# Inverting softmax denominators before their transpose, moving one GpSimd difference a pair forward, and reordering three ScalarE steps at the end of attention

## The chip, the core and the metric

One NeuronCore of one Trainium2 chip runs the whole program. The metric is the device time of one execution in microseconds; "before" is the median of three runs. Engines are named as in the profile: PE (TensorE), PEld (its weight loads), DVE (VectorE), ACT (ScalarE), POOL (GpSimd), SP (SyncE, which only issues DMAs).

## What is computed

Clustered attention over 2 batches, 8 heads, 768 positions and head size 64, and then two gated MLPs on 1536 tokens of width 512 (hidden widths 2048 and 1536):

```python
q_assign = argmax(q_n @ c_n);  k_assign = argmax(k_n @ c_n)
mask   = q_assign[:, :, :, None] == k_assign[:, :, None, :]
scores = where(mask, scale * q @ k.T, -1e9)
attn   = exp(scores - max(scores));  attn /= sum(attn) + 1e-9
x = attn @ v                      # heads side by side: 1536 x 512
h = x @ w_in;  x = (h * sigmoid(h)) @ w_out
out = (sigmoid(x @ w_gate) * (x @ w_val)) @ w_out2
```

## The kernel before

**Attention** goes over 8 pairs p of heads (NPAIR = 8: pairs 0 to 3 are batch b = 0, pairs 4 to 7 batch 1). A pass p has 12 steps, one for each 128 x 768 tile of queries. Step i of pass p issues the scores of the tile two further on (L502, tile s in PSUM, two buffers), so tile 5 of a pair is issued in step 3 and tile 7 in step 5. DVE takes each tile's maximum (L510, `nm`), ACT the exponential with the row's sum (L515, `e`, sums in `tot`), PE turns the result (tiles `t`, L544, and `u`, L531), ACT and DVE copy it out (`ph`, L66 and L69), and PE multiplies by the values (L581, `v`), of which ACT copies one half (L596, `other`) and DVE adds the two (L600, `xf`). PE's order is written out by hand. In attention the order of DVE, ACT, POOL and SP is made by a planner, which places ready instructions by the order in which they were traced; `tc.issue_after(x)` only keeps an instruction behind x in its own engine's queue. Each queue runs in order.

**The next pairs' inputs** are prepared beside this by `prep`: POOL splits q and k in a high and a low part (`qh`, `ql` L431, `kh`, `kl` L434), and DVE picks the clusters: `mk`, `eq`, `wq` (all traced under L456) between the maxima of tiles 4 and 5, and a second `mk` and `oh` after tile 7.

**The end of a pair** is `finish(p)`, a generator that advances by one step in each step of pass p + 1, from step 3 on. For pairs 0 to 5 it waits two steps, then PE turns the 128 x 12 sums to 12 x 128 (L621, `pr`), DVE adds 1e-9 and inverts from PSUM (L627, L628, `rt`), and SP writes `rt` to DRAM and reads it back spread over partitions (L696, L698, `rb`). POOL scales the pair into `acc` (L634). Pair 6 already goes another way: add and reciprocal on the 128 x 12 sums in SBUF (L615, L616, `rs`), then the transpose, then a copy by ACT (L624). Pair 7 has `finish_last`. The three PSUM tiles of `ps_t` are shared by `t`, `u`, `pr` and others.

**POOL also prepares the first MLP's right operands** of batch 0: quarters of `acc` and differences of quarters (`xt1` = b12 - b11 and so on, L648) are rounded (L68) and their remainders taken (L82). They are traced in `finish(3)` behind named POOL instructions, the first difference behind the split of pair 6.

**The MLPs** use a seven-product scheme (`strassen`): x, w, X, y, z, v, W for the first block. X adds to the PSUM bank of x, so it waits until ACT has copied x out (`u2`, L1045). `two` rounds weights on ACT (L66) and takes the remainder on POOL (L880): for the first block `wi0s` and `wi0t` are the sums and differences of its quarters. `right_quarter("x", 1, q, ACT, DVE)` rounds two quarters of batch 1 on ACT and takes their remainders on DVE (L82).

Of the kernel before, what the change touches and what calls it, by code (L numbers as in the profile page):

```python
# [10 lines left out]
F32 = mybir.dt.float32  # L11
# [3 lines left out]
AF = mybir.ActivationFunctionType  # L15
# [17 lines left out]
def clustered_attention_then_two_mlps(ctx, tc, qT, kT, v, cen, cenT, w1i, w1o, w2g, w2v, w2o, out):  # L33
    nc = tc.nc
# [23 lines left out]
    begin = []  # L58
    maxima = []
    copied, latest, moved, firsts, added, paced = [], [], [], [], [], []  # L60
    cast_last = []
    home = {0: xp}

    def cast(eng, o, i):
# [22 lines left out]
    def right_quarter(name, b, q, caster, subber):  # L87
        right_operand(name, b, q, quarters(b)[q], caster, subber, "t1" if q == "12" else None)
# [54 lines left out]
    with ExitStack() as att:  # L143
# [430 lines left out]
        def values(p, j, g, pool=None, apart=False):  # L574
# [29 lines left out]
            one_half()  # L604
            both_halves()

        def finish(p):

            b, hp = divmod(p, HP)
            t = tots.pop(p)  # L610
            early = p == NPAIR - 2
            if early:
                rs = fin.tile([P, 2 * NT], F32, tag="rs", name=f"rs{p}")
                with tc.issue_after(maxima[(p + 1) * 2 * NT + GT + 1].ins):
                    nc.vector.tensor_scalar_add(t, t, 1e-9)  # L615
                    nc.vector.reciprocal(rs, t)  # L616
            else:
                yield
                yield
            pr = ps_t.tile([P, 512], F32, tag="t", name=f"pr{p}")  # L620
            nc.tensor.transpose(pr[0 : 2 * NT, 0:P], rs if early else t, ident)  # L621
            rt = fin.tile([P, P], F32, tag="rt", name=f"rt{p}")
            if early:
                nc.scalar.activation(rt[0 : 2 * NT], pr[0 : 2 * NT, 0:P], AF.Copy)  # L624
            else:
                with tc.issue_after(maxima[(p + 1) * 2 * NT + 2 * GT + 1].ins):
                    nc.vector.tensor_scalar_add(rt[0 : 2 * NT], pr[0 : 2 * NT, 0:P], 1e-9)  # L627
                    nc.vector.reciprocal(rt[0 : 2 * NT], rt[0 : 2 * NT])  # L628
            yield
            rb = fin.tile([P, S], F32, tag="rb", name=f"rb{p}")  # L630
            dma_rows(rb, rt)
            yield
            parts = [t.rearrange("p (h s) -> p h s", h=2) for t in (xf.pop(p), rb)]
            on_pool["scaled", p] = nc.gpsimd.tensor_tensor(acc[:, hp, :, b, :], *parts, op=ALU.mult)  # L634
            yield
            if b < B - 1 and hp == HP - 1:

                def temporary(name):
                    return wk.tile([P, KQ, HS], F32, tag="tt", name=name)

                b11, b21, b12, b22 = quarters(b).values()
                pool = nc.gpsimd
                t = {n: temporary(f"xt{n}{b}") for n in (1, 2)}

                def minus(o, a, c):
                    if o not in t:
                        t[o] = temporary(f"xt{o}{b}")
                    pool.tensor_tensor(t[o], a(), c(), op=ALU.subtract)  # L648

                def operand(n):  # L650
                    right_operand("x", b, f"t{n}", t[n], pool, pool)

                def quarter(q):
                    right_quarter("x", b, q, pool, pool)

                for key, todo in (
                    (("scaled", p), (partial(quarter, "11"), partial(quarter, "21"))),
                    (("split", p + 3), (partial(quarter, "22"), partial(minus, 1, lambda: b12, lambda: b11))),
                    (("scaled", p + 1), (partial(minus, 2, lambda: b22, lambda: t[1]), partial(operand, 1))),
                    (("split", p + 4), (partial(operand, 2), partial(minus, 4, lambda: t[2], lambda: b21))),  # L660
                    (("scaled", p + 2), (partial(operand, 4), partial(minus, 3, lambda: b22, lambda: b12), partial(operand, 3))),
                ):
                    while key not in on_pool:
                        yield
                    for one in todo:
                        with tc.issue_after(on_pool[key].ins):
                            one()
                        yield
# [117 lines left out]
        values(p, 1, 0, ps_t)  # L786
        late, early = turned(p, 1, GT + 1)
        early()
        late()
        late, early = turned(p, 1, GT + 2)  # L790
        late()
# [82 lines left out]
    def two(src, name, pool=None, after=()):  # L874

        w = (pool or buffer(name)).tile([P, 2, src.shape[1]], R32, tag="w", name=f"w{name}")
        hi, lo = w[:, 0], w[:, 1]
        with tc.issue_after(after[0].ins) if after else nullcontext():
            cast(nc.scalar, hi, src)
        nc.gpsimd.tensor_tensor(lo, src, hi, op=ALU.subtract)  # L880
        return hi, lo
# [12 lines left out]
    def scheme(a, b, name, all_four=False):  # L894

        a11, a12, a21, a22 = a[:, 0:Q], a[:, Q:], b[:, 0:Q], b[:, Q:]
        first = two(a, f"{name}a")
        t = wp.tile([P, 4, Q], F32, tag="s", name=f"s{name}", bufs=1)
        sub = nc.gpsimd.tensor_tensor
        sub(t[:, 0], a21, a22, op=ALU.add)  # L900
        sub(t[:, 1], t[:, 0], a11, op=ALU.subtract)
        sub(t[:, 2], a11, a21, op=ALU.subtract)
        sub(t[:, 3], a12, t[:, 1], op=ALU.subtract)
        after = latest if all_four else ()
        s12 = two(t[:, 0:2].rearrange("p a b -> p (a b)"), f"{name}s", after=after)
        s34 = two(t[:, 2:4].rearrange("p a b -> p (a b)"), f"{name}t", after=after)
        last = two(b, f"{name}b") if all_four else two(a22, f"{name}d", dp)
        made = dict(
            a11=part(first, 0),
            a12=part(first, 1),  # L910
            s1=part(s12, 0),
            s2=part(s12, 1),
            s3=part(s34, 0),
            s4=part(s34, 1),
            a22=part(last, 1 if all_four else 0),
        )
        if all_four:
            made["a21"] = part(last, 0)
        return made
# [93 lines left out]
    def strassen(w, name, take, bs, order="xyzwXvW"):  # L1013
# [22 lines left out]
        def column(n):  # L1036
            c[n] = temporary(f"{name}{n}")[:, bs]
            return c[n]

        for n in order:  # L1040
            if n == "x":
                o[n] = bank(f"{name}x", ppa)
                with tc.issue_after(ends[1].ins) if order[1] == "w" else nullcontext():
                    q = run(o[n], "a11", "11")
                nc.scalar.activation(column("u2"), q, AF.Copy)  # L1045
            elif n == "y":
                add(c["u2"], run(bank(f"{name}y"), "s2", "t2"), c["u2"])
            elif n == "z":
# [231 lines left out]
    def steps(main, beside=iter(()), n=None):  # L1280

        for _ in main:
            next(beside, None)
            if n is not None:
                n -= 1
                if n == 0:
                    return
# [18 lines left out]
    weights("1i", 0)  # L1306
    for q in ("11", "12"):
        right_quarter("x", 1, q, POOL, POOL)
    for q in ("21", "22"):
        right_quarter("x", 1, q, ACT, DVE)  # L1310
    front = hidden(0, ONE[0], "xwXyzvW")
    steps(front, n=1)
    look[0] = AHEAD
    weights("1i", 0)
    steps(front, n=5)
# [187 lines left out]
```

## Time and profile before

| | us |
|---|---|
| median of three runs (771.91 to 773.53) | 772.39 |
| the profiled execution | 770.78 |
| its span in the trace | 769.0 |
| PE busy in the span | 755.4 (98%) |
| DVE busy | 601.4 (78%) |
| ACT busy | 427.6 (56%) |
| POOL busy | 385.4 (50%) |

The profiled execution has 1.8 us outside its span. Attention takes the first 240 us, the MLPs the rest. Times in the trace count from the start of the span. "Pass 4" is the time in which pair 4's scores are issued. A number in square brackets at the end of a timeline row is the time that the engine sat idle before that instruction, and what ended it.

### The profile page before, as it was taken

The page shows a single profiled execution, that of the slowest core. Times are in us where ns is not written, and L with a number is a line of the kernel's source. Part 1 is how long each engine was busy: PE and PEld are TensorE (multiplying, and loading weights), DVE is VectorE, ACT ScalarE, POOL GpSimd, SP SyncE. Part 2 cuts the span into 40 slices and gives each one's busy share as a digit, 9 for nine tenths or more (in the row PEclk, how much of TensorE's full clock was granted, in tenths as well). Part 3 has the DMA queues.
Part 4 walks back from the last instruction along what each step waited for, and adds up shares of the span by engine and source line. Part 5 has one row for each costly group of instructions (what it writes and reads, how often), then busy time and mean ns, then how long its engine had stood idle before and what let it go on. Part 6 is the DMA issues. An engine that isn't in the chain of part 4 may idle for free.

```text
span 769.0 us, 11461 instructions
## 1 busy us (share of the span) xinstructions
PE 755.4 (98%) x4289; PEld 648.8 (84%) x4290; DVE 601.4 (78%) x766; ACT 427.6 (56%) x743; POOL 385.4 (50%) x361
## 2 busy tenths in 40 slices
PE   8999999999998999999999999999999999999997
PEld 4766776667766998989989989999998989999896
DVE  6887887797897868798888587996687767858566
ACT  6777776767876763535525346575643624354320
POOL 5335215437465663556646356035785745565430
PEclk9999999999999999999999999999999999999999
DMA  7687458445321131132221111010312212211104
GB/s 210 156 218 186 123 136 206 113 127 126 114 77 55 55 110 56 55 112 102 88 83 56 55 56 55 29 52 32 107 58 87 80 55 83 71 68 55 55 1 165
DMA packets 25487, 71.60 MB, mean 93 GB/s; under 512 B 4484, under 2 KB 4952, under 8 KB 25432
## 3 DMA queue, kind: packets, MB, share of 16 engines
q1 hardware_dynamic: 24888, 70.84, 30.8%
q8 instruction: 34, 0.56, 0.3%
q14 instruction: 21, 0.17, 0.1%
q10 hardware_dynamic: 544, 0.03, 0.0%
HBM read 48.01 MB, written 3.19 MB: 67 GB/s over the span
## 4 chain that ended last, share of the span: by engine, by line
PE 68%; ACT 0%; issue 0%; DVE 0%
PE z L1212 13%; PE y L1142 4%; PE h_0x L1019 4%; PE h_0w L1019 4%; PE g_0x L1019 3%; PE v_0x L1019 3%; PE g_0w L1019 3%; PE v_0w L1019 3%; PE y_00None L1142 2%; PE y_21None L1142 2%; PE y_20None L1142 2%; PE y_11None L1142 2%; PE y_10None L1142 2%; PE y_01None L1142 2%; PE h_0z L1019 2%; PE h_0v L1019 2%
## 5 line engine op out<-in xcount | busy, mean ns | idle before, releaser
L515 ACT ACTIVATE e<-s,nm 128x768 f32<-128x768 f32 x96 | 86.3, 900 | 34.4 <-DVE nm L510 33.8
L510 DVE TENSOR_REDUCE nm<-s 128x1 f32<-128x768 f32 x96 | 90.7, 951 | 12.6 <-PE s L502 10.8
L1212 PE MATMUL z<-wu,ghb 128*128 128x512 f32 (+1 forms) x292 | 89.1, 387 | 0.0
L581 PE MATMUL v<-ph,vv 128*64 128x384 f32 x384 | 69.2, 494 | 0.1
L544 PEld LDWEIGHTS t<-ident,e 128*128 128x128 f32 x384 | 43.1, 140 | 25.6 <-issue 13.8
L1212 PEld LDWEIGHTS z<-wu,ghb 128*128 128x128 f32 x292 | 54.5, 188 | 10.8
L544 PE MATMUL t<-ident,e 128*128 128x128 f32 x384 | 59.9, 279 | 1.8 <-ACT ph L66 1.0
L502 PE MATMUL s<-ka,qa 128*128 128x384 f32 x192 | 57.3, 379 | 0.6 <-ACT e L515 0.5
L1212 PE MATMUL z<-wu,glb 128*128 128x512 f32 (+1 forms) x146 | 56.7, 389 | 0.0
L581 PEld LDWEIGHTS v<-ph,vv 128*64 128x64 f32 x384 | 25.3, 136 | 30.5 <-issue 29.6
L66 ACT ACTIVATE ph<-t 128x512 f32<-128x512 f32 x75 | 43.9, 598 | 12.3 <-PE t L544 11.3
L502 PE MATMUL s<-k,q 128*128 128x384 f32 x192 | 49.9, 339 | 0.4 <-DMA k<-rows 0.4
L634 POOL TENSOR_TENSOR acc<-xf,rb 128x768 f32<-128x768 f32 x7 | 12.9, 1836 | 71.6 <-DMA rb<-d_rb 71.6
L1121 DVE TENSOR_TENSOR acc<-z,acc 128x1024 f32<-128x1024 f32 x24 | 29.2, 1222 | 21.3 <-PE z L1212 21.3
L880 POOL TENSOR_TENSOR wu<-cu,wu 128x512 fp32r<-128x512 f32 x12 | 16.2, 1353 | 51.3 <-ACT wu L66 51.3
L880 POOL TENSOR_TENSOR wo<-co,wo 128x512 fp32r<-128x512 f32 x16 | 22.6, 1417 | 32.8 <-ACT wo L66 32.8
L531 PE MATMUL u<-ident,e 128*128 128x128 f32 x192 | 34.6, 274 | 2.5 <-DVE ph L69 2.3
L600 DVE TENSOR_TENSOR xf<-v,other 64x384 f32<-64x384 f32 x32 | 17.4, 544 | 23.6 <-ACT other L596 23.0
L502 PEld LDWEIGHTS s<-k,q 128*128 128x128 f32 x192 | 34.6, 188 | 1.3 <-DMA k<-rows 0.7
L69 DVE COPY ph<-u 128x512 f32<-128x512 f32 x48 | 32.6, 679 | 1.3 <-PE u L531 1.3
L1142 PE MATMUL y<-gha,wo 128*128 128x384 f32 x128 | 32.8, 334 | 0.0
L1212 PEld LDWEIGHTS z<-wu,glb 128*128 128x128 f32 x146 | 27.4, 188 | 6.0 <-DVE glb L1081 0.5
(711 smaller groups left out, 2147.2 us busy)
## 6 DMA issues: line engine op xcount, KB each, us to landing
ri<-in_w1i SPq DMA_DIRECT2D x16, 512.0 KB, 3.2
ro<-in_w1o SPq DMA_DIRECT2D x16, 512.0 KB, 3.2
ka<-kh SPq DMA_DIRECT2D x32, 192.0 KB, 3.8
rg<-in_w2g SPq DMA_DIRECT2D x12, 512.0 KB, 3.7
rv<-in_w2v SPq DMA_DIRECT2D x12, 512.0 KB, 3.2
ru<-in_w2o SPq DMA_DIRECT2D x12, 512.0 KB, 3.2
qq<-in_qT SPq DMA_DIRECT2D x8, 384.0 KB, 3.2
kk<-in_kT SPq DMA_DIRECT2D x8, 384.0 KB, 5.7
```

Source lines behind the costliest of these rows:

```text
L66: return nc.scalar.activation(o, i, AF.Copy)
L69: return nc.vector.tensor_copy(o, i)
L502: nc.tensor.matmul(s[:, g, 0:HS], lhsT=a[:, j, i * P : (i + 1) * P], rhs=c[:, j, g * HS : (g + 1) * HS], start=n == 0, stop=n == 1,)
L510: maxima.append(nc.vector.tensor_reduce(nm, s[:, :, 0:HS], axis=AX.XY, op=ALU.max, negate=True))
L515: x = nc.scalar.activation(e, s[:, :, 0:HS], AF.Exp, bias=nm, scale=1.0, accum_out=tots[p][:, n : n + 1])
L531: nc.tensor.transpose(both[:, kt - 4, i % 2, :], e[:, kt * P : (kt + 1) * P], ident)
L544: nc.tensor.transpose(t[:, kt, :], e[:, kt * P : (kt + 1) * P], ident)
L581: m = nc.tensor.matmul(o[(L, U)[kt % 2]], lhsT=vv[:, j, kt, :], rhs=ring[:, kt, g * G : (g + 1) * G], start=n < 2, stop=n >= NT - 2,)
L880: nc.gpsimd.tensor_tensor(lo, src, hi, op=ALU.subtract)
L1019: nc.tensor.matmul(o[:, b, 0:HS], lhsT=w[a][s][:, k, :], rhs=right[b, q][t][:, k, :], start=start and k == 0 and n == 0, stop=k == KQ - 1 ...
L1142: nc.tensor.matmul(o[:, d, 0:width], lhsT=s[:, d, k, :], rhs=t[:, c], start=k == 0 and m == 0, stop=k == 1 and m == 2,)
L1212: nc.tensor.matmul(o[:, a, c], lhsT=s[:, q * P : (q + 1) * P], rhs=r[:, c], start=k == 0 and m == 0, stop=k == 1 and m == 2, skip_group_ch ...
```

## The change

Three things are changed. First, `finish` treats pairs 0 to 5 as it treats pair 6: the two empty steps go, the sums are increased and inverted on 128 x 12 in SBUF (behind the maximum of tile 4), then turned, then copied by ACT. Second, the difference b12 - b11 of batch 0, which needs pairs 0 and 1 only, is traced in `finish(2)` right behind that pair's scaling on POOL, no longer in `finish(3)` behind the split of pair 6. Third, ACT's order around the end of attention: the rounding of `wi0t` goes behind the copy of pair 7's second-to-last turned tile (before: behind the last exponential), and the rounding of two quarters of batch 1 goes behind the copy `u2` of the first product x, for which it is traced after that product.

```diff
@@ -58,7 +58,7 @@
-    cast_last = []
+    cast_last, first_u2 = [], []
@@ -604,28 +604,20 @@
+        differences = {}
+
         def finish(p):
             b, hp = divmod(p, HP)
             t = tots.pop(p)
-            early = p == NPAIR - 2
-            if early:
-                rs = fin.tile([P, 2 * NT], F32, tag="rs", name=f"rs{p}")
-                with tc.issue_after(maxima[(p + 1) * 2 * NT + GT + 1].ins):
-                    nc.vector.tensor_scalar_add(t, t, 1e-9)
-                    nc.vector.reciprocal(rs, t)
-            else:
-                yield
-                yield
+            rs = fin.tile([P, 2 * NT], F32, tag="rs", name=f"rs{p}")
+            with tc.issue_after(maxima[(p + 1) * 2 * NT + GT + 1].ins):
+                nc.vector.tensor_scalar_add(t, t, 1e-9)
+                nc.vector.reciprocal(rs, t)
             pr = ps_t.tile([P, 512], F32, tag="t", name=f"pr{p}")
-            nc.tensor.transpose(pr[0 : 2 * NT, 0:P], rs if early else t, ident)
+            nc.tensor.transpose(pr[0 : 2 * NT, 0:P], rs, ident)
             rt = fin.tile([P, P], F32, tag="rt", name=f"rt{p}")
-            if early:
-                nc.scalar.activation(rt[0 : 2 * NT], pr[0 : 2 * NT, 0:P], AF.Copy)
-            else:
-                with tc.issue_after(maxima[(p + 1) * 2 * NT + 2 * GT + 1].ins):
-                    nc.vector.tensor_scalar_add(rt[0 : 2 * NT], pr[0 : 2 * NT, 0:P], 1e-9)
-                    nc.vector.reciprocal(rt[0 : 2 * NT], rt[0 : 2 * NT])
+            nc.scalar.activation(rt[0 : 2 * NT], pr[0 : 2 * NT, 0:P], AF.Copy)
             yield
@@ -633,18 +625,21 @@
             on_pool["scaled", p] = nc.gpsimd.tensor_tensor(acc[:, hp, :, b, :], *parts, op=ALU.mult)
             yield
+            if b < B - 1 and hp == HP - 2:
+                for n in (1, 2):
+                    differences[n] = wk.tile([P, KQ, HS], F32, tag="tt", name=f"xt{n}{b}")
+                b11, _, b12, _ = quarters(b).values()
+                with tc.issue_after(on_pool["scaled", p].ins):
+                    nc.gpsimd.tensor_tensor(differences[1], b12, b11, op=ALU.subtract)
             if b < B - 1 and hp == HP - 1:
...
-                t = {n: temporary(f"xt{n}{b}") for n in (1, 2)}
+                t = differences
@@ -655,7 +650,7 @@
-                    (("split", p + 3), (partial(quarter, "22"), partial(minus, 1, lambda: b12, lambda: b11))),
+                    (("split", p + 3), (partial(quarter, "22"),)),
@@ -786,6 +781,7 @@
         late, early = turned(p, 1, GT + 1)
         early()
+        cast_last[:] = moved
         late()
@@ -903,7 +899,7 @@
-        s34 = two(t[:, 2:4].rearrange("p a b -> p (a b)"), f"{name}t", after=after)
+        s34 = two(t[:, 2:4].rearrange("p a b -> p (a b)"), f"{name}t", after=cast_last if all_four else ())
@@ -1042,7 +1038,7 @@
-                nc.scalar.activation(column("u2"), q, AF.Copy)
+                first_u2[:] = [nc.scalar.activation(column("u2"), q, AF.Copy)]
@@ -1306,10 +1302,11 @@
-    for q in ("21", "22"):
-        right_quarter("x", 1, q, ACT, DVE)
     front = hidden(0, ONE[0], "xwXyzvW")
     steps(front, n=1)
+    with tc.issue_after(first_u2[0].ins):
+        for q in ("21", "22"):
+            right_quarter("x", 1, q, ACT, DVE)
     look[0] = AHEAD
```

## Rows read from the trace of the kernel before

**Rows 1.** The page, part 1: busy time and share of the span.
```profile
PE 755.4 (98%) x4289; PEld 648.8 (84%) x4290; DVE 601.4 (78%) x766; ACT 427.6 (56%) x743; POOL 385.4 (50%) x361
```

**Rows 2.** PE's waits, 20 to 240 us: us in total, times, longest us.
```profile
PE u L531 <- DVE ph L69: 2.3, 3, 1.1
...
PE t L544 <- ACT rt L624: 0.4, 1, 0.4
```

**Rows 3.** Timeline of PE, end of attention: start, us, what.
```profile
235.16 0.66 PE L544 MATMUL t<-ident,e 128*128 128x128 f32 x4 [0.98 <-ACT ph L66]
...
243.73 1.32 PE L1019 MATMUL h_0x<-x,wi0a 128*128 128x384 f32 x6 [1.95 <-ACT h_0u L1045]
```

**Rows 4.** Timeline of PE, passes 3, 4 and 7.
```profile
103.74 0.60 PE L502 MATMUL s<-ka,qa 128*128 128x384 f32 x2
...
106.76 0.62 PE L502 MATMUL s<-ka,qa 128*128 128x384 f32 x2
...
107.57 0.27 PE L621 MATMUL pr<-ident,tot 128*12 128x128 f32 x1
...
130.82 0.60 PE L502 MATMUL s<-ka,qa 128*128 128x384 f32 x2
...
135.36 0.62 PE L502 MATMUL s<-ka,qa 128*128 128x384 f32 x2
...
214.61 0.60 PE L502 MATMUL s<-ka,qa 128*128 128x384 f32 x2
...
218.89 0.62 PE L502 MATMUL s<-ka,qa 128*128 128x384 f32 x2
```

**Rows 5.** Line L456, one form: duration in ns, min/median/max.
```profile
L456 DVE TENSOR_TENSOR wq<-eq,mk x7: 557/557/2105, 27.5 to 188.9; 128x384 bf16<-128x384 bf16 x7
```

**Rows 6.** Timeline of DVE, passes 3, 4 and 5.
```profile
104.72 0.96 DVE L510 TENSOR_REDUCE nm<-s 128x1 f32<-128x768 f32 x1 [0.28 <-PE s L502]
...
131.31 2.10 DVE L456 TENSOR_TENSOR wq<-eq,mk 128x384 bf16<-128x384 bf16 x1
...
158.96 2.00 DVE L456 TENSOR_TENSOR eq<-sim,mk 128x384 bf16<-128x384 f32 x1
```

**Rows 7.** Timeline of POOL, passes 4, 5 and 7.
```profile
130.82 2.18 POOL L648 TENSOR_TENSOR xt<-acc 128x768 f32<-128x768 f32 x1
144.96 1.83 POOL L634 TENSOR_TENSOR acc<-xf,rb 128x768 f32<-128x768 f32 x1 [11.97 <-DMA rb<-d_rb]
...
158.71 1.84 POOL L431 TENSOR_TENSOR ql<-qq,qh 128x768 fp32r<-128x768 f32 x1
...
212.12 1.81 POOL L82 TENSOR_TENSOR xt<-xt,xt 128x768 fp32r<-128x768 f32 x1
```

**Rows 8.** Tile rt: duration in ns, min/median/max, first and last start.
```profile
L627 DVE TENSOR_SCALAR rt<-pr x6: 268/269/270, 55.1 to 193.9; 12x128 f32<-12x128 f32 x6
L628 DVE RECIPROCAL rt<-rt x6: 932/933/933, 55.7 to 194.6; 12x128 f32<-12x128 f32 x6
L624 ACT ACTIVATE rt<-pr x1: 250/250/250, 217.5 to 217.5; 12x128 f32<-12x128 f32 x1
```

**Rows 9.** Tile tot: the add and the reciprocal of pair 6.
```profile
L615 DVE TENSOR_SCALAR tot<-tot x1: 755/755/755, 213.2 to 213.2; 128x12 f32<-128x12 f32 x1
L616 DVE RECIPROCAL rs<-tot x1: 212/212/212, 215.4 to 215.4; 128x12 f32<-128x12 f32 x1
```

**Rows 10.** Timeline of ACT, end of attention.
```profile
233.35 0.63 ACT L66 ACTIVATE wi0t<-si 128x512 fp32r<-128x512 f32 x1
...
241.73 1.58 ACT L66 ACTIVATE x<-acc 128x768 fp32r<-128x768 f32 x2 [1.33 <-issue]
243.21 0.47 ACT L1045 ACTIVATE h_0u<-h_0x 128x384 f32<-128x384 f32 x1
```

**Rows 11.** The chain that ended last, in order of time: start, us, what.
```profile
245.06 1.05 PE h_0y L1019 x6
```

**Rows 12.** Timeline of DVE, end of attention.
```profile
242.60 1.83 DVE L82 TENSOR_TENSOR x<-acc,x 128x768 fp32r<-128x768 f32 x2 [0.96 <-ACT x L66]
```

More of the change, by code (lines that the diff above doesn't have):

```diff
@@ L635, in finish @@
             yield
+            if b < B - 1 and hp == HP - 2:
[4 more added lines that the diff above has]
+                    nc.gpsimd.tensor_tensor(differences[1], b12, b11, op=ALU.subtract)
             if b < B - 1 and hp == HP - 1:
-                def temporary(name):
-                    return wk.tile([P, KQ, HS], F32, tag="tt", name=name)
                 b11, b21, b12, b22 = quarters(b).values()
                 pool = nc.gpsimd
-                t = {n: temporary(f"xt{n}{b}") for n in (1, 2)}
+                t = differences
                 def minus(o, a, c):
                     if o not in t:
-                        t[o] = temporary(f"xt{o}{b}")
+                        t[o] = wk.tile([P, KQ, HS], F32, tag="tt", name=f"xt{o}{b}")
                     pool.tensor_tensor(t[o], a(), c(), op=ALU.subtract)
```

## The prediction

> **What bounds the kernel now.** I read the busy shares first: PE is busy for 98% of the span [rows 1], so only PE's idle time, and work that is put on PE, can move the end. PE's waits come next. After the start of attention they are few: three waits of a `u` transpose for DVE's copy of the one before (2.3 us, the longest 1.1), one for ACT's `rt` copy (0.4) [rows 2], and at the end of attention one of 0.98 us for ACT's `ph` and one of 1.95 us for ACT's `u2` [rows 3]. From there to the end, the chain of work that ended last is PE alone.
>
> A wait shows only part of a loss, so I compared the same stretch of each pass, from the scores of tile 5 to those of tile 7, in PE's timeline [rows 4]: 106.76 - 103.74 = 3.02 us in pass 3 (passes 1 and 2 have the same), 135.36 - 130.82 = 4.54 in pass 4, 218.89 - 214.61 = 4.28 in pass 7. Pass 4 loses 1.5, which is its wait of 1.1 and 0.4 after it. With the same 0.4 behind the other two waits, passes 4 to 6 lose 2.3 + 3 x 0.4 = 3.5 us, passes 5 and 6 thus 2.0. Pass 7 loses 4.28 - 3.02 = 1.26, of which its `pr`, which already stands here, is 0.27 [rows 4]: 1.0.
>
> Why these passes? `wq` takes 557 ns in the median and 2105 at most [rows 5]. The long one, in pass 4, runs from 131.31 to 133.41 [rows 6], while POOL subtracts `xt` from 130.82 to 133.00 [rows 7]. In pass 5 `eq` takes 2.00 us from 158.96 [rows 6], and POOL's `ql` runs from 158.71 to 160.55 [rows 7]; pass 6 has the same pattern once more. DVE then reaches the maximum of tile 5 late, and the exponential and the score buffer of tile 7 wait behind it: in pass 3 tile 7 starts 2.04 us after tile 5's maximum [rows 4, 6]. So DVE operations with two inputs in SBUF stop while POOL reads there. The Trainium skill says the same (SBUF — State Buffer, "Who interferes with whom"): a DVE instruction with two SBUF inputs contends with a GpSimd instruction that reads SBUF, and the later one waits in full. The trace agrees: 2.10 against 0.56 us.
>
> **The difference of quarters.** The subtraction of 2.18 us leaves its place behind pair 6's split, where it meets `wq`, and comes behind the scaling of pair 2 in pass 3. POOL sat idle for 11.97 us before the scaling of pair 3 [rows 7], and idle time of that kind stands before each scaling, so it delays nothing on POOL there. Pass 4 gets back up to 1.5. I leave 0.3 of it, since the split in front ends only at 130.82 [rows 7], 0.5 before `wq`, and so still lies beside `eq`. 1.2.
>
> **The inversion in front, on POOL.** The transpose `pr` moves from step 5 to step 3, that is by 3.02 us [rows 4], and DVE's 0.27 + 0.93 us between it and the DMA are replaced by an ACT copy of 0.25 [rows 8]. So SP issues `rt`'s DMAs 3 to 5 us sooner in six pairs, and POOL's scaling, which waits for them [rows 7], moves by as much. What queues behind it on POOL moves too: in passes 4 to 6 the quarters, differences and remainders, with q and k splits among them. In pass 5 `ql` has to come 1.6 us sooner to be clear of `eq` [rows 6, 7]; 3 us are enough, unless the load of the next q or k holds it. That gives passes 5 and 6 their 2.0 us, bounds 0 and 2.0. In pass 7 POOL's last subtraction ends at 213.93 [rows 7], and holds DVE's add for 755 ns [rows 9] and the weight conversions behind it; 3 us sooner, this is gone: 0.8, bounds 0 and 1.0. SP has nothing queued behind these DMAs that would now wait longer.
>
> **The inversion in front, on DVE and PE.** Behind tile 7 DVE loses 1.2 us of work per pair [rows 8]. PE did not wait there, so that is worth nothing. Between the maxima of tiles 4 and 5 it gets an add and a reciprocal. The reciprocal is 0.21 [rows 9]; a clean add of this form does not show. Its lower bound is the reciprocal's 0.21, its upper the 0.755 of pair 6 [rows 9]; I take the 0.27 of the add from PSUM [rows 8], the nearest that nothing held, so 0.48 together. DVE idles 0.28 there [rows 6], and the maximum of tile 5 comes 0.2 later, which the loop above hands to tile 7. On PE `pr` now stands in front of tile 7 instead of behind it: 3.02 + 0.27 = 3.29 us from tile 5 to tile 7, more than the 3.02 + 0.2 of the loop, so DVE's delay is covered, and the 0.27 comes back behind tile 7. What stays is that `pr` now waits for the reciprocal, with all of PE's queue (turned tiles, tiles 6 and 7) behind it. PE gets there at 103.74 + 0.81 (a tile's scores: 107.57 - 106.76) and two short transposes, about 104.7 [rows 4]. If DVE puts the two between `mk` and `eq`, PE waits for nothing; if behind `wq`, for 104.44 + 0.48, some 0.25. I take 0.15 for each of six pairs: 0.9. ACT's copy of 0.25 falls in ACT's idle time (it is busy for 56% [rows 1]); where it comes late, PE's next `t`, which shares three PSUM tiles with `pr`, waits (second rival). Less than nothing is excluded, as PE gets no less work. Above, an add that waits as pair 6's did adds 0.755 - 0.27, less what is in the 0.25 already: 0.4 each, 2.4.
>
> The row that speaks against the change is that add: 755 ns for twelve columns, from 213.2 until POOL's subtraction ends at 213.93 [rows 7, 9]. The Trainium skill (the same page and section) lets `tensor_scalar` with source and destination in SBUF take both ports, and so contend with GpSimd; the add of before read PSUM. By that rule every new add meets the split that runs at this place, and the sum would be that of the second rival below.
>
> **ACT's order.** `wi0t`'s rounding, 0.63 us, stands in front of the `ph` copy for which PE waits 0.98 [rows 3, 10]. Behind it, it falls in time in which ACT waits for PE; z, its first reader, comes past 246 us [rows 11]. Gain 0.6, bounds 0 and 0.65. The casts of two quarters of batch 1 (1.58 us) run from 241.73 to 243.31, with `u2` behind them at 243.21 [rows 10]. Product w ends at 243.73 - 1.95 = 241.78 [rows 3], and x 1.05 before [rows 11], at 240.7. ACT was idle from 240.40 to 241.73 [rows 10], so `u2` (0.47) would be done at 241.2, and X would not wait: 1.95. What is late next? The casts lose nothing, as they wait for `acc` until 241.7 anyway, but PE now comes to y sooner. Its product ends at about 241.2 + 2 x 1.05 = 243.3 (with the 0.6 from above), and DVE is at the two remainders until 244.43 [rows 12]. If y's addition comes behind both, v waits for y's bank until about 245.0 instead of 244.35: 0.65 lost. If it comes between them, nothing. I take 0.3, so 1.65, bounds 1.3 and 1.95. The next block reads the two quarters a microsecond or more after they are there.
>
> **Sum.** 1.2 + 2.0 + 0.8 - 0.9 + 0.6 + 1.65 = 5.35 us, all of it PE's idle time; behind 245 us PE never waits, so nothing takes it back. The profiled execution would take 770.78 - 5.35 = 765.4 (span 763.7). It stands 1.6 below the median, so the median becomes 772.39 - 5.35 = 767.0. Best ends: 3.5 + 1.0 + 0.65 + 1.95 = 7.1, so 765.3; worst without a rival: 1.2 + 1.3 - 2.4 = 0.1, so 772.3.
>
> **Rivals.** First, the collisions come back elsewhere: the splits in passes 5 and 6 are held by the loads of q and k, which are not moved, and meet `eq` all the same, and pass 7 keeps its conversions late. Then 2.0 and 0.8 go: gain 2.55, 769.8. Second, each new add waits for POOL's split, or PE's next `t` for the `rt` copy, as once in pass 7 (0.4) [rows 2]: 2.4 in place of 0.9, gain 3.85, 768.5. Third, slower: the planner puts add and reciprocal behind the maximum of tile 5, which is traced ahead of them. Then `pr` waits until 104.72 + 0.96 + 0.48 = 106.2 [rows 6] instead of 104.7, with PE's queue behind it: 1.5 x 6 = 9.0 in place of 0.9, a loss of 2.75, 775.1. It decides from 6.25 / 6 = 1.0 us per pair on. Against it: DVE has 0.28 us of idle time ahead of that maximum, and in pass 7 the add started at 213.2 [rows 9], ahead even of tile 5's scores at 214.61 [rows 4]. Fourth, the change does little: `u2` is early but v waits, the moved POOL work meets other DVE work, and the parts cancel: 772.
>
> **How the numbers follow.** Chances: forecast 0.52, first rival 0.17, second 0.15, third 0.09, fourth 0.07. What differs by less than 0.2% (1.5 us) can't be told from no change. Faster are the first three, less a little for their worst ends: 0.81; same 0.1, slower 0.09. The range goes from the best end, a little below it for the spread of the runs, to above the first rival's time: 764.9 to 770.6; the third and fourth rival lie outside.
>
> **What would show it.** Right: `wq` and `eq` at about 0.56 us in all passes; no wait of `u` for `ph` in passes 4 to 6; tile 5 to tile 7 at 3.3 to 3.5 us in all of passes 1 to 7; X of the first block without a wait; the `t` at the end waiting 0.4 instead of 0.98. Wrong: `pr` waiting a microsecond for the reciprocal, `nm` of tile 5 in front of the add, a long `oh` beside POOL's scaling, a new wait of v for its bank, or the clean passes 1 to 3 getting longer by more than 0.4 us each.

## The result and the profile after

The changed kernel takes 763.6 us (median of four runs, 763.23 to 763.81), the kernel before 772.15 (four runs, 770.74 to 773.53, three of them those of the table ahead). The ratio is 0.989, with a 95% interval of 0.987 to 0.9907: 8.5 us faster. The forecast was 767.0 with a range of 764.9 to 770.6. The sign was right; the time lies 1.3 us below the range, and the gain is 1.6 times the forecast 5.35.

| | before | after |
|---|---|---|
| median | 772.15 | 763.6 |
| spread of the runs (highest - lowest) | 2.8 | 0.6 |
| profiled execution | 770.78 | 763.57 |
| its span | 769.0 | 761.6 |

The two traces differ by 7.4 us of span, the medians by 8.5: the profiled execution of before was one of its fast ones, that of after stands at its median.

Five waits of PE are left between 20 and 240 us, and none starts behind that; these three lie at the end of attention, and the `u` waits of [rows 2] are gone (us in total, times, longest us):

```profile
PE h_0v L1015 <- DVE h_0u L1029: 0.6, 1, 0.6
PE t L544 <- ACT ph L66: 0.5, 1, 0.5
...
PE h_0x L1015 <- ACT h_0u L1041: 0.3, 1, 0.3
```

PE's timeline after, passes 3 and 4 and tile 5 of pass 7, answers to [rows 4] (start, us, what):

```profile
103.49 0.59 PE L502 MATMUL s<-ka,qa 128*128 128x384 f32 x2
...
104.49 0.27 PE L618 MATMUL pr<-ident,rs 128*12 128x128 f32 x1
105.18 0.59 PE L502 MATMUL s<-ka,qa 128*128 128x384 f32 x2
...
106.53 0.59 PE L502 MATMUL s<-ka,qa 128*128 128x384 f32 x2
...
109.91 0.59 PE L502 MATMUL s<-ka,qa 128*128 128x384 f32 x2
...
130.45 0.59 PE L502 MATMUL s<-ka,qa 128*128 128x384 f32 x2
...
133.50 0.61 PE L502 MATMUL s<-ka,qa 128*128 128x384 f32 x2
...
210.51 0.60 PE L502 MATMUL s<-ka,qa 128*128 128x384 f32 x2
```

The scores at 103.49, 105.18, 106.53 and 109.91 are those of tiles 5, 6, 7 and 8. From tile 5's to tile 7's it is now 3.04 us in pass 3 and 3.05 in pass 4, where it was 3.02 and 4.54; the forecast had 3.3 to 3.5 here, so that sign did not come. This stretch in all passes, from the same rows of both traces:

| us, pass | 1 | 2 | 3 | 4 | 5 | 6 | 7 |
|---|---|---|---|---|---|---|---|
| tile 5 to tile 7, before | 3.02 | 3.03 | 3.02 | 4.54 | 4.10 | 3.88 | 4.28 |
| tile 5 to tile 7, after | 3.05 | 3.05 | 3.04 | 3.05 | 3.04 | 3.05 | 3.05 |
| tile 7 to the next pass's tile 5, before | 24.05 | 24.06 | 24.06 | 24.04 | 24.05 | 23.18 | |
| the same, after | 23.92 | 23.93 | 23.92 | 23.93 | 23.92 | 23.07 | |

The reason stands in the cluster line and in the inversion's tiles (ns, min/median/max). The 2105 ns of [rows 5] is gone, and every `rt` is ACT's copy:

```profile
L456 DVE TENSOR_TENSOR eq<-sim,mk x7: 547/557/559, 26.9 to 184.0; 128x384 bf16<-128x384 f32 x7
L456 DVE TENSOR_TENSOR wq<-eq,mk x7: 534/540/557, 27.4 to 184.6; 128x384 bf16<-128x384 bf16 x7
...
L620 ACT ACTIVATE rt<-pr x7: 267/267/267, 50.9 to 211.8; 12x128 f32<-12x128 f32 x7
...
L615 DVE TENSOR_SCALAR tot<-tot x7: 162/164/599, 49.0 to 209.1; 128x12 f32<-128x12 f32 x7
```

POOL's timeline: the difference stands behind the scaling of pair 2, and POOL's last remainder ends at 206.16 instead of 213.93 [rows 7]:

```profile
112.64 1.89 POOL L633 TENSOR_TENSOR xt<-acc 128x768 f32<-128x768 f32 x1
...
204.30 1.86 POOL L82 TENSOR_TENSOR x<-acc,x 128x768 fp32r<-128x768 f32 x1
```

At the end of attention, PE's timeline after (it answers to [rows 3]):

```profile
228.90 0.66 PE L544 MATMUL t<-ident,e 128*128 128x128 f32 x4 [0.47 <-ACT ph L66]
...
235.88 1.34 PE L1015 MATMUL h_0x<-x,wi0a 128*128 128x384 f32 x6 [0.35 <-ACT h_0u L1041]
...
239.88 1.31 PE L1015 MATMUL h_0v<-xt,wi0b 128*128 128x384 f32 x6 [0.58 <-DVE h_0u L1029]
241.03 4.32 PE L1087 MATMUL p<-x,wi0a 128*128 128x384 f32 x24
```

and the same product `p` in the timeline of before, which no row above shows:

```profile
248.05 4.33 PE L1091 MATMUL p<-x,wi0a 128*128 128x384 f32 x24
```

PE's lead over before is 5.72 us at the last tile's scores (229.51 against 223.79), 243.73 - 235.88 = 7.85 at X, and 248.05 - 241.03 = 7.02 at `p`: v gives 0.8 back. ACT's and DVE's timelines say why X and v still wait:

```profile
234.17 0.63 ACT L66 ACTIVATE wo<-co 128x512 fp32r<-128x512 f32 x1 [1.93 <-DVE co L851]
...
235.34 0.49 ACT L1041 ACTIVATE h_0u<-h_0x 128x384 f32<-128x384 f32 x1
```

```profile
237.53 1.83 DVE L82 TENSOR_TENSOR x<-acc,x 128x768 fp32r<-128x768 f32 x2 [0.96 <-ACT x L66]
239.27 0.55 DVE L1029 TENSOR_TENSOR h_0u<-h_0y,h_0u 128x384 f32<-128x384 f32 x1
```

ACT's queue holds a rounding of `wo`, the first output weights, that waits 1.93 us for DVE, in front of `other` (at 234.82) and of `u2` (`h_0u`). And y's addition on DVE comes behind both remainders, at 239.27, while v waits for it.

### The profile page after: what moved, and what is told of

The parts are those of the page before. It is cut to its first block, busy times and chain, and to the rows that moved or that the text cites. A ratio compares the mean times of both kernels' runs of the same rounds, so it can differ in the third digit from the quotient of the medians.

```text
span 761.6 us, 11483 instructions
## 1 busy us (share of the span) xinstructions
PE 752.4 (99%) x4289; PEld 648.8 (85%) x4290; DVE 593.1 (78%) x766; ACT 429.2 (56%) x749; POOL 389.2 (51%) x361
## 3 DMA queue, kind: packets, MB, share of 16 engines
HBM read 48.01 MB, written 3.19 MB: 67 GB/s over the span
## 4 chain that ended last, share of the span: by engine, by line
PE 68%; DVE 0%; ACT 0%; issue 0%
PE z L1208 13%; PE y L1138 4%; PE h_0w L1015 4%; PE h_0x L1015 4%; PE g_0w L1015 3%; PE v_0x L1015 3%; PE g_0x L1015 3%; PE v_0w L1015 3%; PE y_00None L1138 2%; PE y_21None L1138 2%; PE y_20None L1138 2%; PE y_11None L1138 2%; PE y_10None L1138 2%; PE y_01None L1138 2%; PE h_0v L1015 2%; PE h_0z L1015 2%
## 5 line engine op out<-in xcount | busy, mean ns | idle before, releaser
L876 POOL TENSOR_TENSOR wo<-co,wo 128x512 fp32r<-128x512 f32 x16 | 24.3, 1518 | 32.9 <-ACT wo L66 32.9
```

## Experiments

Gains are against runs of the kernel before on the same chip; its medians there were 771.4 to 771.9 us. The ratio is not the quotient of the two medians, from which it lies up to 0.0015 away.

| kernel | median us | runs, lowest to highest | ratio to before (95%) | span of its trace |
|---|---|---|---|---|
| inversion only | 766.79 | 6, 766.0 to 767.9 | 0.9948 (0.9932 to 0.9964) | 765.8 |
| difference only | 769.96 | 10, 768.5 to 771.8 | 0.9989 (0.9975 to 1.0002) | 766.7 |
| ACT's order only | 768.8 | 10, 767.6 to 769.6 | 0.9969 (0.9958 to 0.9981) | 767.4 |
| changed, with DVE's load put back | 763.66 | 4, 763.5 to 765.4 | 0.9914 (0.9892 to 0.9936) | 761.7 |
| changed, `wo` behind `u2` | 763.02 | 4, 762.8 to 763.2 | 0.9895 (0.9877 to 0.9913) | 761.2 |
| changed, inversion behind `wq` | 770.49 | 10, 770.1 to 771.1 | 0.9986 (0.9975 to 0.9997) | 768.4 |
| `wo` behind `u2`, a remainder later | 763.17 | 5, 762.7 to 763.4 | 0.9888 (0.9868 to 0.9908) | 761.3 |
| changed, once more | 763.52 | 5, 763.0 to 763.9 | 0.9895 (0.9877 to 0.9913) | 761.1 |
| `wo` behind `u2`, a cast ordered | 762.98 | 4, 762.5 to 763.0 | 0.989 (0.9873 to 0.9908) | 761.2 |
| `wo` behind `u2`, t1's cast later | 763.1 | 5, 762.2 to 763.2 | 0.9885 (0.9866 to 0.9904) | 760.8 |

The three parts alone gain 4.6, 1.5 and 2.6 us by their medians, together 8.7; the whole change gains 8.5. By the ratios they gain 4.0, 0.8 and 2.4, together 7.2, and the whole 8.1 to 8.6. So they add up, within the spread of the runs. Two more kernels, with work added on POOL, have a trace and one time each.

### The inversion alone

```diff
-            else:
-                yield
-                yield
...
-            nc.tensor.transpose(pr[0 : 2 * NT, 0:P], rs if early else t, ident)
+            nc.tensor.transpose(pr[0 : 2 * NT, 0:P], rs, ident)
...
+            nc.scalar.activation(rt[0 : 2 * NT], pr[0 : 2 * NT, 0:P], AF.Copy)
```

> Only the inversion in front, for pairs 0 to 5; the difference of quarters and ACT's order stay as before. Theory (each collision of POOL and DVE costs its own pass): pass 4 keeps its loss, tile 5 to tile 7 about 4.5 us, because xt still runs behind pair 6's split beside wq; passes 5, 6 and 7 come down to about 3.05, passes 1 to 3 gain 0.12 each. Sum 0.12 x 4 + 1.2 + 0.95 + 1.6 = 4.2 us, so about 768. Rival (POOL's backlog is one chain, and the difference in its old place holds it): passes 5 to 7 keep 1 us or more of their losses, gain under 2 us.

Measured: 4.6 us. Tile 5 to tile 7 takes 3.05 us in every pass but pass 4, where it takes 4.59 and a `u` waits 1.09 for DVE. Pass 4 in the timelines of DVE and POOL:

```profile
130.39 2.08 DVE L456 TENSOR_TENSOR wq<-eq,mk 128x384 bf16<-128x384 bf16 x1
```
```profile
129.80 2.26 POOL L638 TENSOR_TENSOR xt<-acc 128x768 f32<-128x768 f32 x1
```

`wq` is held until the subtraction ends at 132.06. So the inversion clears passes 5, 6 and 7, and pass 4 is left to the difference.

### The difference alone

```diff
+            if b < B - 1 and hp == HP - 2:
...
+                with tc.issue_after(on_pool["scaled", p].ins):
+                    nc.gpsimd.tensor_tensor(differences[1], b12, b11, op=ALU.subtract)
...
-    (("split", p + 3), (partial(quarter, "22"), partial(minus, 1, lambda: b12, lambda: b11))),
+    (("split", p + 3), (partial(quarter, "22"),)),
```

> Only the difference b12 - b11 behind pair 2's scaling; inversion and ACT's order as before. Theory: pass 4 comes down from 4.54 to about 3.05 us from tile 5 to tile 7, passes 5 to 7 keep their losses; gain 1.5 us, about 770.7. Rival: with one operation less in POOL's backlog, passes 5 and 6 are freed too, gain 3 us or more.

Measured: 1.5 us by the medians, 0 to 1.9 by the interval, so the time alone does not show a gain. Tile 5 to tile 7, from pass 1 on, takes 3.02, 3.08, 3.03, 3.05, 3.89, 3.66 and 4.30 us: pass 4 is clean, passes 5 to 7 keep their losses. In pass 5 the old collision is there: DVE's `eq` takes 1.79 us from 157.00, and POOL's `ql` runs from 156.55 to 158.38.

So the difference clears pass 4 and no other, as the inversion clears the others and not pass 4.

### ACT's order alone

```diff
-        s34 = two(t[:, 2:4].rearrange("p a b -> p (a b)"), f"{name}t", after=after)
+        s34 = two(t[:, 2:4].rearrange("p a b -> p (a b)"), f"{name}t", after=cast_last if all_four else ())
...
-    for q in ("21", "22"):
-        right_quarter("x", 1, q, ACT, DVE)
...
+    with tc.issue_after(first_u2[0].ins):
+        for q in ("21", "22"):
+            right_quarter("x", 1, q, ACT, DVE)
```

> Only ACT's order at the end of attention. Theory: gain 0.5 us at the last turned tile and 0.85 net at X and v (1.6 less at X, 0.7 more at v), 1.4 us together, about 770.8; attention's passes as before to 0.02 us. Rival: the wait of v is a consequence of the other parts (everything in attention sooner), then v does not wait and the gain is 2.1 us or more.

Measured: 2.6 us, above the 1.4 of the theory and in the rival's range, and yet v, which did not wait before, waits here too. The `t` waits 0.45, X 0.33 (PE's timeline):

```profile
245.66 1.34 PE L1020 MATMUL h_0v<-xt,wi0b 128*128 128x384 f32 x6 [0.58 <-DVE h_0u L1034]
```

So v's wait comes from the order itself and not from the earlier end of attention. The span of this trace is 1.6 us below that of before; what the medians show above that is taken up at "The level of the run". In this execution passes 4 to 7 took 4.28, 3.99, 3.18 and 4.88 us, against 4.54, 4.10, 3.88 and 4.28 in the trace of before: nothing of those passes was changed, yet pass 6 lost 0.16 here and 0.86 there. How long two operations collide differs from one execution to the next.

### DVE's load put back behind tile 7

The changed kernel, with 1.2 us of reciprocals that nobody reads on DVE where the inversion had been.

```diff
+        def load_on_dve(p):
...
+            with tc.issue_after(maxima[(p + 1) * 2 * NT + 2 * GT + 1].ins):
+                nc.vector.reciprocal(idle[0 : 2 * NT, 0, 0 : P // 4], ident[0 : 2 * NT, 0 : P // 4])
+                nc.vector.reciprocal(idle[0 : 2 * NT, 1], ident[0 : 2 * NT])
...
+                    if p < NPAIR - 2:
+                        work.append(load_on_dve(p))
```

> The changed kernel, with 1.2 us of idle reciprocals put back on DVE behind tile 7 in passes 1 to 6, where the old add and reciprocal stood; nothing reads them. Theory (the 0.12 us that every pass gained come from the place of pr on PE): each pass as long as in the changed kernel, same time to 0.2 us. Rival (they come from DVE's relief): each of six passes 0.1 us longer or more, 0.7 us together.

Measured: 763.66 us, as the changed kernel. Tile 7 to the next tile 5 takes 23.92 to 23.96 us, against 23.92 without the load and 24.05 in before. So of the 0.13 us that every pass gained here, at most 0.04 is DVE's relief. What is left is `pr`'s place. These are the scores of tiles 6 and 8 in before, beside those of tiles 5 and 7 in [rows 4]:

```profile
105.32 0.60 PE L502 MATMUL s<-ka,qa 128*128 128x384 f32 x2
...
110.28 0.60 PE L502 MATMUL s<-ka,qa 128*128 128x384 f32 x2
```

| us, pass 3 | tile 5 to 6 | 6 to 7 | 7 to 8 |
|---|---|---|---|
| before | 1.58 | 1.44 | 3.52 (with `pr`) |
| after | 1.69 (with `pr`) | 1.35 | 3.38 |

Behind tile 7 `pr` cost 0.14 us of PE, in front of tile 6 it costs 0.11, and from tile 6 to tile 7 PE gets 0.09 back.

### A subtraction again behind pair 6's split

```diff
+                def extra():
+                    again = wk.tile([P, KQ, HS], F32, tag="again", name="again", bufs=1)
+                    pool.tensor_tensor(again, b12, b11, op=ALU.subtract)
...
+                    (("split", p + 3), (partial(quarter, "22"), extra)),
```

> The changed kernel with one more subtraction b12 - b11 on POOL, into a tile that nothing reads, at the place from which the difference was taken away (behind pair 6's split). Theory (POOL and DVE meet there): eq or wq of pass 4 takes about 2 us, tile 5 to tile 7 there 4.3 to 4.6 us, all other passes 3.05; 1.5 us slower than the changed kernel. Rival (what freed pass 4 is the shorter POOL queue as a whole, or PE's new order): pass 4 stays below 3.3.

Measured: 764.66 us, span 762.6: by this one run 1.1 above the changed kernel, not 1.5. Pass 4 takes 4.33 us, the others 3.05. The collision is back, but it meets another instruction. DVE, POOL and PE in pass 4:

```profile
129.89 1.88 DVE L615 TENSOR_SCALAR tot<-tot 128x12 f32<-128x12 f32 x1
```
```profile
129.86 1.88 POOL L647 TENSOR_TENSOR again<-acc 128x768 f32<-128x768 f32 x1
```
```profile
132.51 0.27 PE L618 MATMUL pr<-ident,rs 128*12 128x128 f32 x1 [0.90 <-DVE rs L616]
```

The new add of twelve columns takes 1.88 us and ends with the subtraction, `eq` and `wq` keep their 0.55 and 0.53, and `pr` waits 0.90. This is the second rival's mechanism, in one pass. By the Trainium skill (SBUF — State Buffer, "Who interferes with whom") `tensor_scalar` can take both ports and then meets GpSimd. The 1.88 against 0.16 us agrees.

### Memsets in its place

The same edit with `for _ in range(3): pool.memset(again, 0.0)` in `extra`: POOL as long, but only writing.

> The same place, but three memsets of that tile, together about 2.2 us by the memsets at the kernel's start (0.74 each), in place of the subtraction: POOL is as busy, but reads nothing. Theory (DVE's second input and POOL's reads share a way, as the Trainium skill has it, SBUF, Who interferes with whom): eq and wq stay at 0.56, pass 4 at 3.05. Rival (any work of POOL holds DVE): pass 4 as long as with the subtraction, above 4.2.

Measured: 763.0 us, span 761.1. Pass 4 takes 3.19 us. DVE and POOL in pass 4:

```profile
129.53 1.12 DVE L615 TENSOR_SCALAR tot<-tot 128x12 f32<-128x12 f32 x1
...
130.84 0.49 DVE L456 TENSOR_TENSOR wq<-eq,mk 128x384 bf16<-128x384 bf16 x1
```
```profile
129.90 2.32 POOL L648 MEMSET again<- 128x768 f32 x3
```

POOL is busy until 132.22, and `wq` takes 0.49 us beside it. The add is held to 130.65: first beside pair 6's split, which runs on POOL until 129.95, then to about the end of the first memset (129.90 + 2.32 / 3 = 130.67). `eq`, which stands behind the add, starts at 129.90 and takes 0.76, until the add is done. So the memsets left `wq`, which has two inputs, alone, and held the add for one memset.

### `wo`'s rounding behind `u2`

```diff
-            job(("1o", i, e), plain, w1o[i, e], f"o{i}_{e}", () if i else moved)
+            job(("1o", i, e), plain, w1o[i, e], f"o{i}_{e}", () if i else first_u2)
```

> The changed kernel with the rounding of the first two output weights (wo) on ACT behind the copy u2. Theory (one of the two waits for DVE's conversion and stands in front of the last other, and so of u2, acc and y's addition): X waits 0 instead of 0.35, v 0 instead of 0.58, gain 0.9 to 1.1 us on PE, about 762.6. Rival (v waits because DVE takes y's addition behind both remainders): v still waits 0.5, gain 0.4 or less.

Measured: X and v wait for nothing, and `y` starts at 248.67 instead of 250.39 us; less the 0.29 by which this execution is ahead at the last tile's scores, that is 1.4 gained. But the second half of `y` now waits (PE's timeline):

```profile
258.84 0.44 PE L1138 MATMUL y<-gla,wo 128*128 128x384 f32 x1 [1.02 <-DVE gla L1077]
```

The median is 0.5 us lower, which this comparison can't tell from nothing. Of the 1.4 gained, 1.0 is given back.

### Which order makes that wait

The first orders, on top of `wo` behind `u2`, the remainder of `p`'s first gated result behind the one of W.

```diff
-            split(g, m, (slice(0, 2), b), f"a{i}", nc.vector)
+            split(g, m, (slice(0, 2), b), f"a{i}", nc.vector, put_behind if m == 0 else None)
...
+    with tc.issue_after(parted[0].ins):
+        put_behind.pop()()
```

> The kernel with wo behind u2, and DVE's remainder of the next block's first result (768 wide, read late) placed behind the remainder of W's result, for which y waited 1.0 us there. Theory (that order on DVE alone made the wait): y waits for nothing; 1.0 us less than with wo behind u2 alone, 1.3 to 1.5 less than the changed kernel, about 762.1. Rival (DVE is short of time there, and something else is late next): gain under 0.5 over wo behind u2 alone.

Measured: 763.17 us, and `y` waits the same 1.02. My cause was wrong: the wait is for the remainder of `p`'s second result.

The second orders a cast of batch 1's sums on ACT behind that result's rounding.

```diff
-    next(rest)
+    with tc.issue_after(rounded[0].ins):
+        next(rest)
```

> The kernel of wo behind u2, with one more edit: ScalarE's rounding of batch 1's first sum (the xt cast that stood at 253.1 us) is ordered behind its rounding of the second gated result of batch 1's directly computed product (gha, which stood at 253.8). In the two runs before, PE waited 1.0 us at 259.1, in the second half of y, for VectorE's remainder gla of that result, which came behind the remainder of xt. Theory (this order alone makes that wait): gla is done near 256 us, y waits for nothing, the end comes 1.0 us sooner than with wo behind u2: span 760.2, median near 762.0. Rival (something else is late in its place: the sums of batch 1, now later, or a weight conversion): a new wait of PE between 260 and 275 us takes over half of it back, median 762.6 to 763.0.

Measured: 762.98 us, the same wait. The cast that this edit orders stood behind already, so no queue changed: the run repeats `wo` behind `u2`. The cast in front is that of the difference t1.

```diff
-    last("x", 1)
+    with tc.issue_after(rounded[0].ins):
+        last("x", 1)
```

> The kernel of wo behind u2 with one more edit. The cast xt that stands at 252.9 us on ScalarE, in front of the gated gha at 253.6, is that of batch 1's difference t1 (the run before had ordered t2's, which stood behind gha anyway, and so changed nothing). Here t1's cast, and with it its remainder on VectorE (2.05 us at 253.8), are ordered behind gha; gla then stands ahead of t1's remainder and of one weight conversion on VectorE. Theory (this order alone makes PE's wait of 1.0 us at 258.9, in the second half of y): gla is done near 256 us, y waits for nothing, span 760.2, median near 762.0. Rival (something else is late in its place: t1's or t2's operands for the next block, or the conversion that now stands further back): a new wait of PE between 260 and 280 us takes over half of it back, median 762.6 to 763.0 or above.

Measured: `y` waits for nothing, since its `gla` now starts at 253.89 on DVE, and a later block waits in its place on PE:

```profile
285.83 0.50 PE L1138 MATMUL y_00None<-gla,wo 128*128 128x512 f32 x1 [0.43 <-DVE gla L1077]
```

The theory on the first wait held, and the trace is 0.4 us shorter; the median (763.1) shows no difference. None of these beats the changed kernel by more than can be measured.

### The inversion behind `wq`

The case of the third rival: add and reciprocal are ordered behind `wq`, and the planner puts the reciprocal behind the maximum of tile 5.

```diff
+            ranked_last[:] = [queued(one, nc.vector.tensor_tensor, wq, eq, ranks, op=ALU.mult)]
...
-            with tc.issue_after(maxima[(p + 1) * 2 * NT + GT + 1].ins):
+            with tc.issue_after(ranked_last[0].ins if p < NPAIR - 2 else maxima[(p + 1) * 2 * NT + GT + 1].ins):
                 nc.vector.tensor_scalar_add(t, t, 1e-9)
                 nc.vector.reciprocal(rs, t)
```

> The changed kernel with the add of pairs 0 to 5 ordered behind wq on DVE; the planner then puts the reciprocal behind tile 5's maximum, the case of my third rival. Theory (pr has to wait for it with PE's queue behind): pr waits 1.2 to 1.5 us in each of six passes, 7 to 9 us in all, about 771. Rival (the tiles behind pr have slack as well): under 0.5 us per pass, 766 or less.

Measured: 770.49 us, 6.9 above the changed kernel. Its waits of PE from 20 to 240 us (the first row), and pass 3 on DVE (lines from L457 on are one further down):

```profile
PE pr L619 <- DVE rs L617: 6.3, 6, 1.1
```
```profile
104.45 0.55 DVE L457 TENSOR_REDUCE mk<-sim 128x24 f32<-128x384 f32 x1
105.04 0.56 DVE L457 TENSOR_TENSOR eq<-sim,mk 128x384 bf16<-128x384 f32 x1
105.63 0.56 DVE L457 TENSOR_TENSOR wq<-eq,mk 128x384 bf16<-128x384 bf16 x1
106.11 0.17 DVE L616 TENSOR_SCALAR tot<-tot 128x12 f32<-128x12 f32 x1
106.47 0.96 DVE L511 TENSOR_REDUCE nm<-s 128x1 f32<-128x768 f32 x1 [0.20 <-PE s L503]
107.34 0.22 DVE L617 RECIPROCAL rs<-tot 128x12 f32<-128x12 f32 x1
```

`pr` waits behind a maximum of 0.96 us, six times (1.06 in pass 3), and pass 3 takes 4.27 us from tile 5 to tile 7. Where two small DVE instructions stand decides 6.9 of the 8.5 us.

### The changed kernel once more

The kernel after, unchanged, to set its spread beside that of before.

> The changed kernel once more, beside the one above on one chip. It should take 763.6 to 0.5 us, and spread by less than 1 us over its runs, where the kernel before spreads by 3 to 4.

Measured: 763.0 to 763.87 us over five runs, before on the same chip 769.66 to 774.01 over eleven.

## Why the prediction was right in sign and too small

The parts of the gain in the span, as forecast and as the two traces show them:

| term | forecast | measured | from |
|---|---|---|---|
| passes 4 to 6, the collisions | 1.2 + 2.0 = 3.2 | 3.4 | tile 5 to the next tile 5: 1.60 + 1.19 + 0.94, less 0.11 each |
| pass 7 | 0.8 | 1.6 | 4.28 - 3.05, and 0.39 from tile 7 to the last tile's scores |
| inversion on DVE and PE | -0.9 | +0.7 | 0.11 in each of six passes: 0.13 from tile 7 to tile 5, less 0.02 from 5 to 7 |
| ACT's order: `t` and X | 0.6 + 1.95 | 0.54 + 1.59 | the lead 5.72 at the last scores, 6.26 at x, 7.85 at X |
| ACT's order: v | -0.3 | -0.74 | the lead 7.85 at X, 246.99 - 239.88 = 7.11 at v |
| later | 0 | 0.3 | 7.06 at the last product, 7.4 in the span |
| sum | 5.35 | 7.4 | |

**The collisions: right.** `wq` and `eq` are at 0.54 to 0.56 us in all passes, and the parts run alone show which edit clears which pass. The first rival (collisions come back elsewhere) did not occur.

**The inversion on DVE and PE: the step that failed.** I took 0.15 us a pair for a `pr` that waits, 0.9 in all, and wrote: "Less than nothing is excluded, as PE gets no less work." Both are wrong: `pr` waits for nothing, and the six passes gain 0.7. This is DVE's timeline after, in pass 3:

```profile
102.46 0.55 DVE L456 TENSOR_REDUCE mk<-sim 128x24 f32<-128x384 f32 x1
102.93 0.17 DVE L615 TENSOR_SCALAR tot<-tot 128x12 f32<-128x12 f32 x1
103.05 0.56 DVE L456 TENSOR_TENSOR eq<-sim,mk 128x384 bf16<-128x384 f32 x1
103.52 0.22 DVE L616 RECIPROCAL rs<-tot 128x12 f32<-128x12 f32 x1
103.66 0.54 DVE L456 TENSOR_TENSOR wq<-eq,mk 128x384 bf16<-128x384 bf16 x1
104.47 0.96 DVE L510 TENSOR_REDUCE nm<-s 128x1 f32<-128x768 f32 x1 [0.28 <-PE s L502]
```

The two new instructions lie between `mk`, `eq` and `wq`, each of which reads the one before. From `mk` to `eq` and from `eq` to `wq` it is 0.59 and 0.61 us, start to start; with nothing between, in the run with the inversion behind `wq`, 0.59 and 0.59. So they cost DVE 0.02 us at most, `nm` still waits 0.28 for PE as in [rows 6], and `pr` finds `rs` ready.

PE has the same instructions, but not the same time. I added `pr`'s whole 0.27 to the 3.02 us from tile 5 to tile 7 and came to 3.29; it is 3.05. `pr` costs 0.11 there and not 0.27, and the 3.02 us were not all work of PE: in ACT's timeline of before the exponential of tile 5 ends at 106.71, and tile 7's scores, which need its buffer, start 0.05 behind it. PE stood in front of them for a moment that is too short for the list of waits, and `pr` now fills it: of its 0.11, the 0.09 from tile 6 to tile 7 come back. So the loop from tile 5's maximum to tile 7 that the prediction names hid part of the cost, and behind tile 7 the 0.14 is saved. This is read from the two traces; of the runs, only the load put back on DVE bears on it, by leaving at least 0.09 of the 0.13. The sign of the bound was an argument, not a row.

**Pass 7: right mechanism, half the size.** I counted the held add and left the conversions at a little. I also took 0.27 out for the `pr` that stands here, though the stretch takes 3.05 us with the same `pr` after, and did not look behind tile 7, where 0.39 more are gained. DVE's timeline before:

```profile
214.66 0.82 DVE L851 TENSOR_SCALAR ci<-ci 128x512 int32<-128x512 int32 x1 [0.70 <-POOL ci L840]
...
216.86 0.95 DVE L510 TENSOR_REDUCE nm<-s 128x1 f32<-128x768 f32 x1
```

A conversion waits for POOL, which is late, and stands with two more in front of the maximum of tile 5: it starts 216.86 - 214.61 = 2.25 us after the tile's scores. After, `nm` starts 0.99 us after them (211.50 against 210.51 in DVE's and PE's timelines), having waited for PE.

**ACT's order: right for `t`, too much for X and v.** "`u2` (0.47) would be done at 241.2, and X would not wait" left out what else stands in front of `u2`: a `wo` rounding that waits 1.93 us for DVE (rows of after, above). X keeps 0.35. The order alone shows both waits, and `wo` behind `u2` takes them away. v lost 0.74; I had seen it with bounds of 0 and 0.65 and taken the middle; it came out a little beyond the worse one.

**The level of the run.** "It stands 1.6 below the median, so the median becomes 772.39 - 5.35" carried an offset over that the changed kernel doesn't have: its profiled execution stands at its median. Without that the forecast would have been 765.4, and its range, lowered by the same 1.6, 763.3 to 769.0: the result lies in it, 0.3 above its lower end. Of the 3.4 us between 767.0 and 763.6, 1.6 are this and 1.8 the sum.

TensorE's granted clock says where most of that offset comes from. In one trace, that of the inversion alone, it falls in mid-run. First PE's timeline, then windows of 1 us, in which the number behind PE's busy time is the granted clock:

```profile
238.94 1.71 PE L1009 MATMUL h_0x<-x,wi0a 128*128 128x384 f32 x6 [1.95 <-ACT h_0u L1035]
240.45 2.12 PE L1009 MATMUL h_0y<-xt,wi0s 128*128 128x384 f32 x6
...
244.79 4.32 PE L1081 MATMUL p<-x,wi0a 128*128 128x384 f32 x24
```
```profile
240.00:241.00 1.00, 1.00 (x5) 0.50 0.00 0
...
242.00:243.00 1.00, 1.00 (x4) 0.50 0.00 0
```

From 240 to 243 us it is 0.50, the lower of its two levels (1.2 and 2.4 GHz), right behind X's wait of 1.95 us. From X to `p` it takes 5.85 us, against 248.05 - 243.73 = 4.32 in before: 1.5 lost. Before and the difference alone have the same wait in their traces and no fall, so it comes in some executions only. The mean granted clock is on record for every run of the changed kernel and of the experiments, and for the runs of before beside the latter. With ACT's order of before (before, inversion only, difference only) 38 of 77 runs are at 0.997 or 0.998; with the changed order none of 53 is below 0.999. The runs of before at 0.997 or 0.998 average 772.4 us, its others 770.8, and the profiled execution of before (770.78) is at 1.000. So the prediction put a part of the gain at nothing: with X's wait, ACT's order takes away a fall of the clock that about half of the executions had. One trace shows the fall and its place; for the other runs the place is inferred from their means.

This also fits ACT's order alone, whose 2.6 us by the medians become 1.9 against the 12 runs of before on that chip at 0.999 or more. It is one part of the spread. The other seems to be the collisions: at 0.999 or more before still spreads by 2.6 us, and ACT's order alone, which keeps the collisions, by 2.1; the kernels without collisions spread by about 1 or less, but for one run of 765.4 with the load put back. A collision's length changes between executions, as pass 6 with ACT's order alone showed. That this makes the rest of the spread is argued, not shown.

**Rivals.** The second (adds that wait for POOL's split) touched pass 4 only, with 599 ns, and cost nothing there; with a subtraction put back it was 1.88 us. The third was a matter of order alone: with the inversion behind `wq` it cost 1.2 us a pass, not 1.5, and 6.9 in all. With the gains that were left it ended at 770.5 and not at 775.1.

## What to carry to other kernels

In a chain of DVE instructions that each read the one before, look at the start-to-start time against the duration: a short independent instruction placed between them can be free, and the same instruction behind the chain can come to stand behind a longer one and make PE wait. Before adding an instruction's duration to a stretch, ask whether the stretch is the engine's own work or a loop through other engines with room in it. An offset between a profiled execution and the median belongs to that kernel's spread: compare the granted clocks of the two, and don't carry the offset to a kernel from which its cause may be taken away. And when an engine's order is changed to release a wait, read the whole queue in front of the released instruction, including those that themselves wait, since the next one in line takes the wait over.

## What the runs showed of the hardware that was not expected

- Two short DVE instructions between dependent ones cost next to nothing: `mk` to `eq` 0.59 us with an add of 0.17 between them and 0.59 without, `eq` to `wq` 0.61 with a reciprocal of 0.22 and 0.59 without.
- One PE transpose of 0.27 us took 0.11 us of PE's time between two `u` transposes (1.69 against 1.58), and 0.14 between scores and values (3.52 against 3.38).
- While POOL only wrote (three memsets, 2.32 us), `wq` took 0.49 us, while it took 2.08 beside a subtraction; an add in SBUF took 1.12 and 1.88 us beside them, and 0.16 alone.
- Behind a wait of PE of 1.95 us the granted clock was 0.50 from 240 to 243 us in one trace, and 1.00 behind the same wait in two others.
- With the collisions and that wait gone, the spread of the runs fell from 4.4 us (eleven runs) to 0.9 (five).
